# Two transformer layers on one core: woven work cut into stages by engine, and the last product's operands loaded three groups ahead

## The chip, the cores and the metric

The kernel runs on one core of one Trainium2 chip. A core has a matrix engine (PE; its weight loads are listed apart as PEld), a vector engine (DVE), a scalar engine (ACT), GpSimd (POOL) and SyncE (SP), which issues the transfers. Each engine takes its instructions strictly in the order of its own queue; semaphores tie the queues together. The metric is device time in microseconds (us): the median of several executions. One further execution was profiled, and its trace is what the prediction reads.

## The reference

The input x is one sequence of S = 2048 rows of D = 576. Two layers are applied with the same weights, each an attention and an MLP:

```
def attention(x):                      # H = 32 heads of 18
    q, k, v = split_heads(x @ wqkv)
    phi_q = concat([softmax(q @ w_phi), softmax(-(q @ w_phi))])
    phi_k = concat([softmax(k @ w_phi), softmax(-(k @ w_phi))])
    kv, z = phi_k.T @ v, sum(phi_k, rows)
    return ((phi_q @ kv) / (phi_q @ z + 1e-6)) @ wo
def mlp(x):                            # F = 4608
    return (relu(x @ w1 + b1) ** 2) @ w2 + b2
for _ in range(2):
    x = x + attention(layernorm(x))
    x = x + mlp(layernorm(x))
```

Everything is float32.

## The kernel before, in words

**Tiles.** The 2048 rows are four blocks of 512 (`TB`), a block is four tiles of 128 (`NT`). D is cut in pieces of 128 and F in 36 groups of 128 (`NF`). A float32 operand is held as a high and a low part, and a product is three matmuls: high by high, low by high, high by low. So each operand needs a "split": ACT copies the high part, and DVE or POOL subtracts it to make the low one.

**Stages.** A layer first needs the sums over all keys (`kv`), then does each block's queries, attention and MLP. In time: a barrier that finishes the keys; the MLP of one block, group by group (`g_mlp`, names `m_3` in layer 0 and `m_1` in layer 1), into which the attention of the next block and the queries and features of the third are woven (`back_first`); the MLP of the second block (`m_2` and `m_0`), into which the rest of the attention of blocks three and four is woven (`back_second`); then both MLPs of blocks three and four together (`g_pair`, names `m_p`). Their first product is made out of seven products in place of eight, which needs sums of blocks of rows: the "combined rows" t1 to t4, b11, b21 and b22, made by `g_norm_halves` and `g_norm_second` (L893 to L932 of the page). Eighteen steps of `products` do these (three PSUM banks: bx, by and bz), and the second product of one of the two blocks alongside. `seconds` then does the other block's second product: 36 groups of 15 matmuls (L1031 and L1041), whose hidden rows come back from memory (`load_high`, L1079 to L1083) and whose weights are loaded and split by `load_wide` (L996 to L1002). In layer 0 the second layer's norm, values and keys of three blocks (`back_keys`, names `n_`, `v_`, `k_`, `w_`, `kv_`) are woven into `seconds`.

**What sets the order.** `weave(main, other, rate)` writes out the order of the program: after each step of `main` it adds `rate` to an account and runs steps of `other`, each of which takes its cost from the account, while there is one unit in it. Rates and costs are constants in the code. A scheduler then keeps each engine's instructions in about the order written. A step of `other` writes out all that it needs on every engine, one after the other: a key tile's step (`g_k` with `soft_k`) writes the matmuls of the raw key, DVE's maximum and minimum (L427, L428), the subtractions (DVE L431, POOL L432), the exponential (ACT L433), the sums and reciprocal (DVE L435, L436), the scaling (POOL L443) and at once or one step later the `kv` matmuls (L471). A query tile's features are made by `g_soft` (the same to L436) and `g_phi`: products with the key sums (L589, one half on DVE and one on POOL), their reduction (L590), small rows (L591 to L594) and the scaling (L599, one half on DVE, one on POOL). The combined rows of a tile are one step: PE's transposes into a PSUM bank (L823), the sums on DVE and POOL (to L912), and five splits (ACT L922, DVE or POOL L923).

**Buffers.** While an MLP is woven, two PSUM banks (tag "w") are free for the woven work; in `seconds` three. In `seconds` the loads of group f + 2 are written behind the matmuls of group f, with two buffers each for the raw weights (`r2`), their split (`s2`) and the hidden rows' split (`hb`). In the woven MLPs, a group is the relu (ACT L731), a square and its split (ACT L732 and L733, DVE L734) between its first product (L724) and its second (L742 and L751), and the splits of its weights (ACT L709 and L710, DVE L712 and L713, POOL L714).

Of the kernel before, what the change touches and what calls it, by code (L numbers as in the profile page):

```python
# [21 lines left out]
def layers_kernel(  # L22
# [304 lines left out]
    def g_norm(x_of, dst, name, then=None):  # L327
# [15 lines left out]
        def turn(t, xn):  # L343
# [4 lines left out]
            pt = wtile(f"{name}p{t}")  # L348
            p3 = pt.rearrange("p (c n) -> p c n", n=P)
            for c in range(KC):  # L350
                nc.tensor.transpose(p3[:, c], xn[:, c * P : (c + 1) * P], ident)
# [3 lines left out]
        def turn_rest(h):  # L355

            xh = dst["h"]
            rows = slice(h * TB // 2, (h + 1) * TB // 2)
            pt = wtile(f"{name}p{NT}{h}")
            for i in range(NT // 2):  # L360
                nc.tensor.transpose(pt[:, i * P : (i + 1) * P],
                                    xd[:, h * NT // 2 + i].rearrange("p a b -> p (a b)"), ident)
            nc.scalar.activation(xh[:, KC, rows], pt[:, : TB // 2], AF.Copy)
            nc.vector.tensor_sub(xh[DT:, KC, rows], pt[DT:, : TB // 2], xh[DT:, KC, rows].bitcast(F32))

# [5 lines left out]
        yield from lagged(NT, scale, turn_all)  # L371
# [47 lines left out]
    def soft(src, name, apart=False):  # L419
# [12 lines left out]
        nc.gpsimd.tensor_sub(e4[:, 1], m[:, 1], v)  # L432
        nc.scalar.activation(e, e, AF.Exp)  # L433
        r = sb.tile([P, 2, H], F32, tag="r", name=f"{name}r", bufs=4)
        nc.vector.tensor_reduce(r, e4, op=ALU.add, axis=AX.X)  # L435
        nc.vector.reciprocal(r, r)  # L436
        return e, r

    def soft_k(src, name):
        e, r = soft(src, name)  # L440
        e3 = e.rearrange("p s (h d) -> p (s h) d", d=DH)
        r2 = r.rearrange("p s h -> p (s h)")
        nc.gpsimd.tensor_mul(e3, e3, r2.unsqueeze(2).to_broadcast([P, 2 * H, DH]))  # L443
# [137 lines left out]
    def g_phi(layer, er, ph, name, fine=False):  # L581

        zb = sums[layer]["zb"]
        for t in range(NT):
            e, r = er[t]
            u = sb.tile([P, 2, H], F32, tag="u", name=f"{name}u{t}")
            for s in range(2):
                m = sb.tile([P, D], F32, tag="qk" if fine else "x", name=f"{name}m{t}{s}", bufs=5)
                (nc.gpsimd if s else nc.vector).tensor_mul(m, e[:, s], zb[:, s])  # L589
                nc.vector.tensor_reduce(u[:, s], m.rearrange("p (h d) -> p h d", d=DH), op=ALU.add, axis=AX.X)  # L590
            nc.vector.tensor_mul(u, u, r)  # L591
            nc.vector.scalar_tensor_tensor(u[:, 0], u[:, 0], DEN_EPS, u[:, 1], op0=ALU.add, op1=ALU.add)
            nc.vector.reciprocal(u[:, 1], u[:, 0])
            nc.vector.tensor_mul(r, r, u[:, 1].unsqueeze(1).to_broadcast([P, 2, H]))  # L594
            if fine:
                yield
            for s in range(2):
                e3 = e[:, s].rearrange("p (h d) -> p h d", d=DH)
                (nc.gpsimd if s else nc.vector).tensor_mul(  # L599
                    e3, e3, r[:, s].unsqueeze(2).to_broadcast([P, H, DH]))  # L600
            ph.append(e)
            yield

# [197 lines left out]
    def g_norm_halves(x_of, name, then, main, tail, cost):  # L801
# [16 lines left out]
        for t in range(NT):  # L818
            pt = wtile(f"{name}p{t}")
            p4 = pt.rearrange("p (a c n) -> p a c n", a=2, n=P)  # L820
            for a in range(2):
                for c in range(HK):
                    nc.tensor.transpose(p4[:, a, c], xns[t][:, (a * HK + c) * P : (a * HK + c + 1) * P], ident)  # L823
            main(t, p4)
            yield cost
            if t % 2:
                pt = wtile(f"{name}p{NT}{t}")
                p3 = pt[:TP].rearrange("p (a n) -> p a n", a=2)
                for a in range(2):
                    for i in range(2):  # L830
                        nc.tensor.transpose(p3[:, a, i * P : (i + 1) * P],
                                            xd[:, t - 1 + i, a * TP : (a + 1) * TP], ident)
                tail(t // 2, p3)
                yield cost

    def g_norm_first(x_of, dst, name, then):
# [17 lines left out]
        yield from g_norm_halves(x_of, name, then, main, tail, 1.0)  # L854
# [4 lines left out]
    def g_norm_second(x_of, dst, name, then):  # L859

        ops, full = {}, []
# [53 lines left out]
        def main(t, p4):  # L915
# [4 lines left out]
            for k, src in combine((p4[:, 0], p4[:, 1]), *old):  # L920
# [4 lines left out]
        def tail(h, p3):  # L925
            cols = slice(h * TB // 2, (h + 1) * TB // 2)
            for k, src in combine((p3[:, 0], p3[:, 1]), *([f[:, cols]] for f in full)):
# [3 lines left out]
        yield from g_norm_halves(x_of, name, then, main, tail, 5.0)  # L931
        dst.update(ops)  # L932

    def g_pair(layer, blocks, x, after, name):
# [61 lines left out]
        def load_wide(f):  # L996
            r2 = sb.tile([P, D], F32, tag="r2", name=f"{name}r2_{f}")
            nc.sync.dma_start(r2, w2[(f % NF) * P : (f % NF + 1) * P])
            s2 = sb.tile([P, NC * HP], F32R, tag="s2", name=f"{name}s2_{f}")
# [77 lines left out]
        def load_high(f):  # L1077
            r = sb.tile([P, TB], F32, tag="ft", name=f"{name}g{f}", bufs=4)
            nc.sync.dma_start(r, hd[f % NF])  # L1079
            hb = sb.tile([P, 2 * D], F32R, tag="hb", name=f"{name}hc{f}")  # L1080
# [258 lines left out]
```

## Time and profile before

| what | number |
|---|---|
| median of three executions | 2571.31 us (2571.26 to 2573.71) |
| the profiled execution's own time | 2576.0 us |
| its span in the trace | 2574.2 us |
| PE busy | 2493.8 us, 97% |
| DVE, ACT, POOL busy | 64%, 51%, 38% |
| PE waits, barrier and start of the program among them | about 80 us |

The page's first part gives busy times, its second the span in 40 slices; below that, groups of instructions by line. The line numbers are those of the kernel before; the same code stands further down in the changed one (L471 is L527 there, L1041 is L1142). "Waits" are idle times of an engine put down to the instruction that released it.

### The profile page before, as it was taken

To read this page: it belongs to the slowest core of one execution; us is meant where nothing else is said; L and a number is where in the kernel's file an instruction comes from. 1 tells how busy PE (TensorE), PEld (TensorE's weight loads), DVE (VectorE), ACT (ScalarE), POOL (GpSimd) and SP (SyncE) were. 2 spreads that over 40 slices of the span, in tenths; PEclk is the share of its full clock that TensorE was granted. 3 is DMA by queue.
4 is the path that set the end of the run, shared out by engine and by line. 5 is a ranking of instruction groups with operands and counts; after the bars stand their busy time and mean duration, and the time that the engine had idled before them with its cause. 6 is when DMAs were issued, how large, how long until landed. Compare 5 with 4: busy or idle time off the path is not lost. (4 is left out here: it accounts for less than half of the span.)

```text
span 2574.2 us, 41588 instructions
## 1 busy us (share of the span) xinstructions
PE 2493.8 (97%) x15108; PEld 2185.5 (85%) x15108; DVE 1640.9 (64%) x2570; ACT 1303.3 (51%) x2293; POOL 973.6 (38%) x1101
## 2 busy tenths in 40 slices
PE   8998999999999999999899989999999999999999
PEld 8998888888887888888888988888888877888888
DVE  7778757655856655545777778475658565555444
ACT  4344545354536666654343435553455466666543
POOL 3544312312434555541334433132123345555322
PEclk9999999999999999999999999999999999999999
DMA  8103433345334433338543143233453344333265
GB/s 251 57 23 107 141 90 85 109 132 183 99 112 125 136 111 102 107 97 256 166 139 116 45 143 104 85 92 110 137 173 94 117 127 146 100 108 102 86 195 156
DMA packets 257224, 312.99 MB, mean 122 GB/s; under 512 B 29818, under 2 KB 175482, under 8 KB 254458
## 3 DMA queue, kind: packets, MB, share of 16 engines
q1 hardware_dynamic: 255760, 307.64, 39.4%
q8 instruction: 118, 1.93, 0.3%
q10 hardware_dynamic: 1258, 2.70, 0.3%
q14 instruction: 88, 0.72, 0.1%
HBM read 255.42 MB, written 54.82 MB: 121 GB/s over the span
## 5 line engine op out<-in xcount | busy, mean ns | idle before, releaser
L1002 POOL TENSOR_TENSOR m_ps<-m_pr,m_ps 128x128 fp32r<-128x128 f32 x144 | 120.0, 834 | 343.5 <-ACT m_ps L1000 289.4
L1001 DVE TENSOR_TENSOR m_ps<-m_pr,m_ps 128x448 fp32r<-128x448 f32 x144 | 97.0, 674 | 153.0 <-ACT m_ps L1000 153.0
L1041 PE MATMUL m_pacc<-m_ps,m_phb 128*128 128x448 f32 x864 | 188.5, 366 | 0.0
L1041 PEld LDWEIGHTS m_pacc<-m_ps,m_phb 128*128 128x128 f32 x864 | 162.1, 188 | 18.1
L1000 ACT ACTIVATE m_ps<-m_pr 128x576 fp32r<-128x576 f32 x144 | 97.9, 680 | 142.6 <-PE m_pacacc L1031 86.1
L1041 PE MATMUL m_pacacc<-m_ps,m_phc 128*128 128x448 f32 x648 | 147.2, 370 | 0.0
L1041 PEld LDWEIGHTS m_pacacc<-m_ps,m_phc 128*128 128x128 f32 x648 | 122.9, 190 | 10.6
L751 PE MATMUL m_2acc<-m_2s,m_2hb 128*128 128x448 f32 x432 | 100.3, 366 | 2.9 <-DVE m_2hb L734 2.9
L751 PE MATMUL m_0acc<-m_0s,m_0hb 128*128 128x448 f32 x432 | 100.1, 366 | 2.8 <-DVE m_0hb L734 2.8
L724 PE MATMUL m_0ph<-a_0nh,m_0h 128*128 128x512 f32 (+1 forms) x380 | 98.0, 385 | 4.8 <-ACT m_0hr L731 4.7
L724 PE MATMUL m_2ph<-a_2nh,m_2h 128*128 128x512 f32 (+1 forms) x380 | 98.9, 387 | 3.4 <-ACT m_2hr L731 3.3
L724 PE MATMUL m_1ph<-t1onh,m_1h 128*128 128x512 f32 (+1 forms) x380 | 99.3, 390 | 0.6 <-ACT t1onh L352 0.6
L751 PE MATMUL m_3acc<-m_3s,m_3hb 128*128 128x448 f32 x432 | 99.7, 366 | 0.0
L751 PE MATMUL m_1acc<-m_1s,m_1hb 128*128 128x448 f32 x432 | 99.4, 365 | 0.0
L724 PE MATMUL m_3ph<-t0onh,m_3h 128*128 128x512 f32 (+1 forms) x380 | 97.3, 385 | 1.4 <-DVE t0ox L681 1.4
L751 PEld LDWEIGHTS m_2acc<-m_2s,m_2hb 128*128 128x128 f32 x432 | 81.0, 188 | 14.3 <-DVE m_2hb L734 3.8
L751 PEld LDWEIGHTS m_0acc<-m_0s,m_0hb 128*128 128x128 f32 x432 | 80.9, 188 | 14.0 <-DVE m_0hb L734 3.7
L751 PEld LDWEIGHTS m_1acc<-m_1s,m_1hb 128*128 128x128 f32 x432 | 81.0, 188 | 10.4
L751 PEld LDWEIGHTS m_3acc<-m_3s,m_3hb 128*128 128x128 f32 x432 | 81.0, 188 | 10.5 <-ACT m_3hb L732 0.2
L724 PEld LDWEIGHTS m_0ph<-a_0nh,m_0h 128*128 128x128 f32 x380 | 68.0, 188 | 18.7 <-ACT m_0hr L731 6.1
L724 PEld LDWEIGHTS m_2ph<-a_2nh,m_2h 128*128 128x128 f32 x380 | 68.7, 190 | 17.3 <-ACT m_2hr L731 4.5
L724 PEld LDWEIGHTS m_1ph<-t1onh,m_1h 128*128 128x128 f32 x380 | 70.8, 195 | 14.4 <-ACT t1onh L352 0.8
(2504 smaller groups left out, 7423.8 us busy)
## 6 DMA issues: line engine op xcount, KB each, us to landing
m_pr<-in_B_w SPq DMA_DIRECT2D x144, 288.0 KB
m_pr<-in_B_w SPq DMA_DIRECT2D x72, 256.0 KB
hd<-m_pu SPq DMA_DIRECT2D x72, 256.0 KB
m_pg<-hd SPq DMA_DIRECT2D x72, 256.0 KB
m_3r<-in_B_w SPq DMA_DIRECT2D x36, 288.0 KB
m_2r<-in_B_w SPq DMA_DIRECT2D x36, 288.0 KB
m_1r<-in_B_w SPq DMA_DIRECT2D x36, 288.0 KB
m_0r<-in_B_w SPq DMA_DIRECT2D x36, 288.0 KB
```

The costliest lines, as they stand in the source:

```text
L724: nc.tensor.matmul(ph[:, cols], a, m, start=(k == 0), stop=(k == len(ops) - 1))
L751: nc.tensor.matmul(acc[t][:, :R], a[:, rows], m, start=(f == 0 and k == 0), stop=(f == NF - 1 and k == 2))
L1000: nc.scalar.activation(s2[:, :D], r2, AF.Copy)
L1001: nc.vector.tensor_sub(s2[:, D : D + R], r2[:, :R], s2[:, :R].bitcast(F32))
L1002: nc.gpsimd.tensor_sub(s2[:, D + R : 2 * D], r2[:, R:], s2[:, R:D].bitcast(F32))
L1041: nc.tensor.matmul(accs[b][t][:, :R], a[:, rows], m, start=(g == 0 and k == 0), stop=(g == NF - 1 and k == 2))
```

## The change

The arithmetic is the same but for one operation; the order of the program, the stages' costs and some buffers change.

1. A helper `pipeline(n, stages, costs)` runs item i's stage k at step i + k, the latest stage first, with a weave step between any two.
2. The features of queries (`g_features`) become five stages: start, exponential, sums and products, factors, scaling; 10.0 units a tile.
3. The combined rows become stages: transposes (0.3), sums (3.6), splits (2.4), over six items (four tiles and two pairs of tails); `g_norm_first` transposes (0.3) and splits (1.0).
4. In `products`, z is made by ACT from bx with the bias as soon as the first of two products is done, and DVE adds by to it after the second; before, ACT copied by and DVE added bx and the bias.
5. `back_keys`: norm in stages; keys as raw, start, exponential, end, an empty step, `kv`; woven at 4.0 a group, before 4.5.
6. `seconds`: the loads of group f + 3 are written ahead of the matmuls of group f. Of the groups of the last product (f from 36 on) every odd one has its raw weights in tag r1 and its split in tag h1; of its hidden rows' splits every odd one lies in two constants that are free by then (kbh, kbl).

```diff
+    def pipeline(n, stages, costs):
+        for i in range(n + len(stages) - 1):
+            for k in reversed(range(len(stages))):
+                if 0 <= i - k < n:
+                    stages[k](i - k)
+                    yield costs[k]
...
     def g_features(layer, raws, ph, name):
-        er = []
-        yield from paced(held(g_soft(raws, er, name)), 5.5)
-        yield from paced(held(g_phi(layer, er, ph, name, True)), 2.8)
+        rs, ms = {}, {}
+        def start(t):
+            ph.append(soft_parts(raws[t], f"{name}Q{t}"))
+        def add(t):
+            rs[t] = soft_sums(ph[t], f"{name}Q{t}")
+            ms[t] = phi_products(layer, ph[t], f"{name}m{t}")
+        def factors(t):
+            phi_factors(ms.pop(t), rs[t], f"{name}u{t}")
+        yield from held(pipeline(NT, (start, lambda t: soft_exp(ph[t]), add, factors, lambda t: phi_scale(ph[t], rs[t])),
+                                 (2.6, 0.4, 3.0, 2.8, 1.2)))
...
-        yield from g_norm_halves(x_of, name, then, main, tail, 1.0)
+        yield from g_norm_halves(x_of, name, then, (main,), (tail,), (0.3, 1.0))
...
-        yield from g_norm_halves(x_of, name, then, main, tail, 5.0)
+        yield from g_norm_halves(x_of, name, then, (main, split_main), (tail, split_tails), (0.3, 3.6, 2.4))
...
                 product(k, bx, "a11", "b11", True)
+                z = sb.tile([P, TB], F32, tag="hr", name=f"{name}z{f0}", bufs=2)
+                nc.scalar.activation(z, bx, AF.Identity, bias=bias(f0))
                 product(k, by, "a12", "b21", True)
-                z = sb.tile([P, TB], F32, tag="hr", name=f"{name}z{f0}", bufs=2)
-                nc.scalar.activation(z, by, AF.Copy)
-                nc.vector.scalar_tensor_tensor(z, bx, bias(f0), z, op0=ALU.add, op1=ALU.add)
+                nc.vector.tensor_add(z, by, z)
                 nc.scalar.activation(z, z, AF.Relu)
...
-            for f in range(NF, NF + 2):
+            for f in range(NF, NF + 3):
                 load_wide(f)
                 load_high(f)
             for f in range(NF, 2 * NF - 1):
+                if f + 3 < 2 * NF:
+                    load_wide(f + 3)
+                    load_high(f + 3)
                 second(f)
-                if f + 2 < 2 * NF:
-                    load_wide(f + 2)
-                    load_high(f + 2)
                 yield
...
-                    yield from paced(g_k(xk, wpair("k", f"w{m}"), es, f"k{m}",
-                                         then=lambda t: kv_tile(1, vts[t], es[t], f"kv{m}_{t}")), 3.2)
+                stages = (raw, start, lambda t: soft_exp(es[t]), end, lambda t: None)
+                if not last:
+                    stages += (lambda t: kv_tile(1, vts[t], es[t], f"kv{m}_{t}"),)
+                yield from pipeline(NT, stages, (1.0, 2.6, 0.4, 1.8, 0.1, 0.8))
...
-        weave(seconds, iter(()) if layer else back_keys(), 4.5)
+        weave(seconds, iter(()) if layer else back_keys(), 4.0)
```

Three places show what moves. The first is PE in `seconds` of layer 0, at the keys of block 3: `m_pacacc` and `m_pach` are the groups of the last product (the numbers after `m_ps` count the groups), `kv_3_2k` is the `kv` product of tile 2. Before:

```order
L471 MATMUL kv_3_2k<-k_3K2e,vs_12017 32x2x18 x32
L1041 MATMUL m_pach<-m_ps_46_12682,m_phc_12688 128x448 x3
L1041 MATMUL m_pacacc_11963<-m_ps_46_12682,m_phc_12688 128x448 x3
L1041 MATMUL m_pacacc_11964<-m_ps_46_12682,m_phc_12688 128x448 x3
L1041 MATMUL m_pacacc_11965<-m_ps_46_12682,m_phc_12688 128x448 x3
L1031 MATMUL m_pacacc_11966<-m_phc_12688,m_ps_46_12682 128x512 x3
L1041 MATMUL m_pach<-m_ps_47_12741,m_phc_12747 128x448 x3
L1041 MATMUL m_pacacc_11963<-m_ps_47_12741,m_phc_12747 128x448 x3
L1041 MATMUL m_pacacc_11964<-m_ps_47_12741,m_phc_12747 128x448 x3
L471 MATMUL kv_3_3k<-k_3K3e,vs_12018 32x2x18 x32
L1041 MATMUL m_pacacc_11965<-m_ps_47_12741,m_phc_12747 128x448 x3
```

The same place in the changed kernel, from the end of group 45, which follows the last raw key:

```order
L1132 MATMUL m_pacacc_11966<-m_phc_12504,m_ps_45_12498 128x512 x3
L527 MATMUL kv_3_0k<-k_3K0e,vs_12026 32x2x18 x32
L1142 MATMUL m_pach<-m_ps_46_12567,m_phc_12573 128x448 x3
L1142 MATMUL m_pacacc_11963<-m_ps_46_12567,m_phc_12573 128x448 x3
L1142 MATMUL m_pacacc_11964<-m_ps_46_12567,m_phc_12573 128x448 x3
L1142 MATMUL m_pacacc_11965<-m_ps_46_12567,m_phc_12573 128x448 x3
L1132 MATMUL m_pacacc_11966<-m_phc_12573,m_ps_46_12567 128x512 x3
L527 MATMUL kv_3_1k<-k_3K1e,vs_12027 32x2x18 x32
L1142 MATMUL m_pach<-m_ps_47_12600,m_phc_12606 128x448 x3
```

Group 47 follows whole, and behind it `kv_3_2k` and `kv_3_3k` one after the other. So the `kv` of tiles 0 to 2 have moved behind the last raw key by one to three groups; that of the last tile has three whole groups and three `kv` products between the raw key and itself, where it had two groups and nine matmuls of a third, and one `kv`.

The second place is ACT while the combined rows are made: `a_1n...` are splits of combined rows, `m_2...` the MLP's relu (L731), square (L732, L733) and weights (L709, L710). Before:

```order
L922 ACTIVATE a_1nt1h<-a_1nu_8318 128x2x128
L922 ACTIVATE a_1nh<-a_1nu_8318 128x2x128
L731 ACTIVATE m_2hr_8365<-m_2ph_8277,b1t 128x512
L922 ACTIVATE a_1nh<-a_1np_8313 128x2x128
L922 ACTIVATE a_1nt3h<-a_1nu_8319 128x2x128
L922 ACTIVATE a_1nt4h<-a_1nu_8319 128x2x128
L732 ACTIVATE m_2hb_8366<-m_2hr_8365 128x512
L709 ACTIVATE m_2h_27_8414<-m_2r_27_8408 128x640
```

In the changed kernel, where L1016 is the split and L812 to L814 are relu and square:

```order
L812 ACTIVATE m_2hr_8306<-m_2ph_8218,b1t 128x512
L790 ACTIVATE m_2h_26_8348<-m_2r_26_8342 128x640
L813 ACTIVATE m_2hb_8307<-m_2hr_8306 128x512
L814 ACTIVATE m_2hr_8306<-m_2hr_8306 128x512
L1016 ACTIVATE a_1nh<-a_1np_8254 128x2x128
L1016 ACTIVATE a_1nt1h<-a_1nu_8269 128x2x128
L1016 ACTIVATE a_1nh<-a_1nu_8269 128x2x128
L791 ACTIVATE m_2s_25_8285<-m_2r_25_8279 128x576
L1016 ACTIVATE a_1nt3h<-a_1nu_8270 128x2x128
L1016 ACTIVATE a_1nt4h<-a_1nu_8270 128x2x128
```

A tile's five splits and the relu have changed places: the relu stands ahead of the splits, and the split rows were summed a step earlier.

The third place is DVE while a block's features are made, with the MLP's own rows between (L712 and L713 weights, L734 the square's split). Before, at the start of tile 2's softmax:

```order
L712 TENSOR_TENSOR m_2h_12_7165<-m_2r_12_7159,m_2h_12_7165 128x640
L734 TENSOR_TENSOR m_2hb_7129<-m_2hr_7128,m_2hb_7129 128x512
L427 TENSOR_REDUCE a_1Q2m<-a_1qs_6916 128x32
L428 TENSOR_REDUCE a_1Q2m<-a_1qs_6916 128x32
L713 TENSOR_TENSOR m_2s_11_7107<-m_2r_11_7101,m_2s_11_7107 128x448
L431 TENSOR_TENSOR a_1Q2e<-a_1qs_6916,a_1Q2m 128x576
L435 TENSOR_REDUCE a_1Q2r<-a_1Q2e 128x64
```

In the changed kernel (L793, L794 and L815 are the MLP's rows, L483 the sums, L641 the product with the key sums, L470 to L474 the next tile's start, L656 the scaling):

```order
L793 TENSOR_TENSOR m_2h_14_7290<-m_2r_14_7284,m_2h_14_7290 128x640
L815 TENSOR_TENSOR m_2hb_7248<-m_2hr_7247,m_2hb_7248 128x512
L470 TENSOR_REDUCE a_1Q3m<-a_1qs_6998 128x32
L471 TENSOR_REDUCE a_1Q3m<-a_1qs_6998 128x32
L794 TENSOR_TENSOR m_2s_13_7226<-m_2r_13_7220,m_2s_13_7226 128x448
L474 TENSOR_TENSOR a_1Q3e<-a_1qs_6998,a_1Q3m 128x576
L656 TENSOR_TENSOR a_1Q0e<-a_1Q0e,a_1Q0r 128x576
L647 TENSOR_REDUCE a_1u_7277<-a_1m_7215 128x32
L647 TENSOR_REDUCE a_1u_7277<-a_1m_7216 128x32
```

The sums of a tile (L435, now L483) no longer stand right behind the subtraction that ACT's exponential waits for; other tiles' rows lie between.

More of the change, by code (lines that the diff above doesn't have):

```diff
@@ L584, in g_phi, with phi_scale @@
+    def phi_scale(e, r):
+        for s in range(2):
+            e3 = e[:, s].rearrange("p (h d) -> p h d", d=DH)
+            (nc.gpsimd if s else nc.vector).tensor_mul(
+                e3, e3, r[:, s].unsqueeze(2).to_broadcast([P, H, DH]))
+    def g_phi(layer, er, ph, name):
         for t in range(NT):
             e, r = er[t]
[L586 to L600, printed above, removed]
+            phi_factors(phi_products(layer, e, f"{name}m{t}", "x"), r, f"{name}u{t}")
@@ L798, in g_mlp, with g_norm_halves @@
             nc.sync.dma_start(out[b * TB + t * P : b * TB + (t + 1) * P] if layer else xs[b][t], x)
-    def g_norm_halves(x_of, name, then, main, tail, cost):
+    def g_norm_halves(x_of, name, then, main, tail, costs):
         xd = sb.tile([P, NT, 2 * TP], F32, tag="xd", name=f"{name}e", bufs=1)
@@ L859, in g_norm_second @@
     def g_norm_second(x_of, dst, name, then):
-        ops, full = {}, []
+        ops, full, made = {}, [], {}
         def two(t):
```

162 lines of the change are left out of this document (119 added, 43 removed).

## The prediction

> **What bounds the kernel now.** I read the page's busy times first, then PE's waits, then the stages in which they lie, then their timelines. The page says that PE is busy nearly all the time:
>
> ```profile
> span 2574.2 us, 41588 instructions
> PE 2493.8 (97%) x15108; PEld 2185.5 (85%) x15108; DVE 1640.9 (64%) x2570; ACT 1303.3 (51%) x2293; POOL 973.6 (38%) x1101
> L1041 PE MATMUL m_pacc<-m_ps,m_phb 128*128 128x448 f32 x864 | 188.5, 366 | 0.0
> ```
>
> The change takes no matmul away, so all that it can win lies in the 80.4 us in which PE is idle (2574.2 less 2493.8), and in stretches at a lower clock. PE's waits, with the total, the number and the longest:
>
> ```profile
> PE m_pach L1041 <- DVE m_ps L1001: 5.5, 2, 4.5
> PE m_0ph L724 <- ACT m_0hr L731: 4.7, 4, 2.3
> PE m_ppx L1012 <- DVE m_pz L1108: 3.8, 5, 1.4
> PE m_2ph L724 <- ACT m_2hr L731: 3.3, 2, 2.4
> PE m_ppx L1012 <- DVE m_pu L1122: 3.2, 2, 1.6
> PE kv_0k L471 <- POOL k_3K0e L443: 3.0, 1, 3.0
> PE kv_3k L471 <- POOL k_3K3e L443: 3.0, 1, 3.0
> PE kv_3k L471 <- POOL k_2K3e L443: 3.0, 1, 3.0
> PE m_2acc L751 <- DVE m_2hb L734: 2.9, 2, 1.6
> PE m_0acc L751 <- DVE m_0hb L734: 2.8, 2, 1.6
> ...
> PE m_pach L1041 <- DVE m_phc L1083: 1.2, 3, 0.4
> ...
> PE n_3p L351 <- DVE n_3n L336: 0.8, 1, 0.8
> ...
> PE n_3p L361 <- DVE n_3h L364: 0.6, 1, 0.6
> ...
> PE kv_1k L471 <- POOL k_2K1e L443: 0.2, 1, 0.2
> ```
>
> The waits at the start and in the barriers are left out here; the change doesn't reach them. The rest falls into four groups, one for each part of the change: keys beside the last product (5.5 + 3.0 + 3.0 + 3.0 + 1.2 + 0.8 + 0.6 + 0.2 = 17.3 us in 11 waits); combined rows (the relu's: 4.7 + 3.3 = 8.0 in 6); features (L734's: 2.9 + 2.8 = 5.7 in 4); products (z's: 3.8 in 5). The wait on `m_pu` stays, its code being the same.
>
> A wait costs a little more than its idle time, since the matmul behind it shows its whole length where one in a row shows a step. Nine of them in a row:
>
> ```profile
> 1238.80 2.02 PE L1041 MATMUL m_pacacc<-m_ps,m_phc 128*128 128x448 f32 x9
> 1240.66 0.86 PE L1031 MATMUL m_pacacc<-m_phc,m_ps 128*128 128x512 f32 x3
> ```
>
> One step is (1240.66 - 1238.80) / 9 = 0.207 us and one matmul's length 0.366 (the page's row), so a wait costs 0.16 us more.
>
> Some waits cost still more, for the granted clock falls behind them (the clock is the column behind POOL's). The first two rows follow a wait of `kv_0k` of 3.0 us, the third a wait of 2.4 for a relu, the fourth one of 2.3 for a relu in layer 1:
>
> ```profile
> 1228.20:1231.70 3.50, 3.50 (x74) 3.42 (x75) 1.98 (x4) 1.82 (x3) 1.55 (x2) 0.51 0.07 25
> 1231.70:1235.20 3.50, 3.50 (x26) 3.42 (x25) 2.73 (x5) 1.55 (x4) 1.49 (x2) 1.00 0.30 81
> 787.90:791.40 3.50, 3.50 (x10) 2.75 (x9) 3.04 (x8) 1.88 (x4) 0.91 (x2) 0.51 0.41 104
> 2065.40:2068.80 3.40, 3.40 (x15) 2.80 (x16) 2.56 (x6) 2.30 (x4) 0.46 (x1) 1.00 0.20 56
> ```
>
> 3.5 us at 0.51 lose 1.7 us. [...]
>
> The keys' stage has four such stretches, which its mean clock shows too (0.03 of 235 us is 7):
>
> ```profile
> 1160.00:1395.00 235.00, 217.67 (x1715) 198.13 (x1714) 163.04 (x233) 101.57 (x166) 80.27 (x80) 0.97 0.55 173
> ```
>
> So at most this can go: keys 17.3 + 11 x 0.16 + 4 x 1.7 = 25.9; combined rows 8.0 + 6 x 0.16 + one stretch, about 1.4 = 10.3; features 5.7 + 4 x 0.16 = 6.4; products 3.8 + 5 x 0.16 = 4.6. Together 47.2 us, under 2% of the run.
>
> **The change, part by part.** *Keys and the loads three deep.* The last tile of block 3 shows the chain:
>
> ```profile
> 1245.06 0.78 PE L1041 MATMUL m_pach<-m_ps,m_phc 128*128 128x448 f32 x3
> ...
> 1258.05 0.77 PE L471 MATMUL kv_3k<-k_3K3e,vs 128*32 128x36 f32 x64 [3.01 <-POOL k_3K3e L443]
> 1255.66 2.33 POOL L443 TENSOR_TENSOR k_3K3e<-k_3K3e,k_3K3r 128x1152 f32<-128x1152 f32 x1 [2.91 <-DVE k_3K3r L436]
> ```
>
> From the raw key's last matmul (1245.06) to `kv` it takes 13.0 us. By the order of the changed kernel three groups and three `kv` products lie between: 15 matmuls of 0.207 are 3.1 us, a `kv` about 0.7 (1258.05 to the next at 1258.75), so 3 x 3.1 + 3 x 0.7 = 11.4. Of the wait of 3.0 there remain 1.0 to 1.6, at this tile and its like in block 2; the waits of `kv_0k` and `kv_1k`, whose products move behind later raw keys, are gone. The 4.5 us at L1001 are a weight split that stands on DVE behind a long split of the next block's values:
>
> ```profile
> 1379.17 3.61 DVE L301 TENSOR_TENSOR w_0v0l<-w_0v0r,w_0v0h 128x1440 fp32r<-128x1440 f32 x1
> ...
> 1387.22 0.87 DVE L1001 TENSOR_TENSOR m_ps<-m_pr,m_ps 128x448 fp32r<-128x448 f32 x1
> ACT m_ps L1000 <- PE m_pacacc L1031: 20.4, 5, 7.3
> ```
>
> ACT's part of that split waits for PE to free a buffer (last row). Three deep, it is written a group (3.1 us) and more ahead, and has twice the buffers, so 4.5 becomes at most 1.4. Two tails of about 1.3 with 0.16 and a clock stretch each (2 x 3.2 = 6.4) and 0.5 elsewhere stay: 25.9 - 6.9, so **-19**. The best is -25.9. The worst is that both tail waits stay with their stretches (2 x (3.0 + 0.16 + 1.7) = 9.7), the 4.5 too (6.4), and 2 more come at `n_3n`, whose rows now stand close ahead of their transposes: -8. What is moved past: the transfers of `load_wide` and `load_high` are issued one group earlier on SP, the same number; nothing queued behind them there is waited for sooner.
>
> *Combined rows.* The relu stands on ACT behind a split whose source POOL is still summing:
>
> ```profile
> 793.04 0.74 POOL L912 TENSOR_TENSOR a_1nu<-a_1nu,a_1nb21l 128x256 f32<-128x256 f32 x1
> 793.80 0.42 ACT L922 ACTIVATE a_1nt4h<-a_1nu 128x256 fp32r<-128x256 f32 x1 [1.35 <-POOL a_1nu L912]
> 794.13 0.67 ACT L731 ACTIVATE m_2hr<-m_2ph,b1t 128x512 f32<-128x512 f32 x1
> ...
> 740.00:850.00 110.00, 106.59 (x519) 91.53 (x518) 67.71 (x118) 60.31 (x116) 51.69 (x71) 0.98 0.39 114
> ```
>
> In the changed order the relu is ahead of the splits, and those find sums written a step before. ACT's own rows don't fill the stage (60 of 110 us, last row), so what held the relu was POOL. **-9** of 10.3. If one layer's half stays, -5; beyond that see the slower rival.
>
> *Features.* Here DVE is nearly full. The window of one block's features, a wait of DVE for the exponential, three rows at the end, and a first product of the MLP from the chain of work that ended last:
>
> ```profile
> 630.00:697.00 67.00, 64.06 (x325) 55.93 (x324) 58.85 (x80) 35.21 (x57) 27.19 (x20) 1.00 0.26 77
> DVE a_1Q3r L435 <- ACT a_1Q3e L433: 2.3, 1, 2.3
> 693.16 1.69 POOL L599 TENSOR_TENSOR a_1Q3e<-a_1Q3e,a_1Q3r 128x576 f32<-128x576 f32 x1 [3.75 <-DVE a_1Q3r L594]
> 693.74 1.65 DVE L734 TENSOR_TENSOR m_2hb<-m_2hr,m_2hb 128x512 fp32r<-128x512 f32 x1
> ...
> 697.51 0.68 DVE L734 TENSOR_TENSOR m_2hb<-m_2hr,m_2hb 128x512 fp32r<-128x512 f32 x1
> ...
> 1975.52 3.26 PE m_0ph L724 x14
> ```
>
> The wait for the exponential (2.3 of DVE's 8.15 idle us, with its like at other tiles) goes, since other tiles' rows lie between subtraction and sums. But 44.4 units become 40, at 5.0 a group 8.0 groups for 8.9, with the same DVE rows of the features; the 0.9 group less holds three MLP rows a group of 0.68 (L734 alone) or more, at 0.85 about 2.3 us. So DVE has some 56.5 us to do in 8 groups. PE needs 6.4 for each: 14 matmuls of 512 columns 3.26 (last row), three more of these 0.70, and twelve of 0.207; 51.2 in all. Were it all exposed, a block would lose 5.3, 2.1 more than today's 3.2: over two layers **+5** with rounding. Against that, DVE runs into the stage ahead of PE and can fall behind by some groups' slack before PE sees it, and a row that now lies under a POOL row is stretched (1.65 against 0.68 at L734), which needn't fall on the same rows again. Best -6.4; I take **-4.4**, a left-over of 1 us a block.
>
> [...]
>
> *Products.* z's bank bx is now read by ACT behind the first product, with 14 matmuls (3 us) until PE writes it again; DVE's row, on which PE waited, reads by. That bank is needed only two products later. **-4.5** of 4.6. Worst: the five waits move to ACT's row (0 gained) and one like `m_pu`'s longest (1.6) comes on top.
>
> *New waits* I put at **+2**: the weaves end later (`back_second` 163.6 units for 158.4, at 5.0 a group 32.7 groups for 31.7, of 36), and rows that were hidden meet others.
>
> Sum: -19 - 9 - 4.5 - 4.4 + 2 = -35, so 2576.0 becomes 2541. The medians stand 4.7 below the profiled execution (2571.3), so the forecast is **2536**.
>
> **The rivals.**
> 1. *The waits move on* instead of going: features stay bound by DVE, the tails of the keys and the `n_3n` rows keep most of theirs. Keys -10, combined rows -6, products -3, features +1, others +1: -17, 2554. For it: DVE at 58.85 of 67 us and 163 of 235 in the two stages, and no work is taken from any engine.
> 2. *All of it goes*, 47: 2524. For it: ACT and POOL are at half in these stages. Against it: the 11.4 us for a chain of 13.0.
> 3. *Slower: two banks held too long.* The combined rows' transposes have two PSUM banks. Today a bank is used within one step; now it is held from the transposes over sums and splits, 6.0 units or 1.2 groups, and the transposes of item i need the bank of item i - 2. PE, in order, would stop with the MLP behind it. The price: one step's POOL work that the split must sit out is five rows (two sums, three splits by the code) of 0.74 as at L912, 3.7 us, with 0.16 and a clock stretch 5.6; four items of six, two layers: +45, and the 9 not won, against 35: +19, 2590. It decides from where the split of item i - 2 ends after PE reaches item i. Against it: PE needs 8 us for these 1.2 groups, twice the 3.7.
> 4. *Nothing comes of it*: the scheduler's order would leave the waits as they are, 2571. Against it: the order's rows did move.
>
> **How the numbers follow.** Forecast 0.60 (2536, give or take 8), rival 1 0.22, rival 2 0.06, rival 3 0.08, rival 4 0.04. The range takes the forecast, rival 1 and the upper end of the best case: 2523 to 2558; the worst ends of all four parts (-8, -5, +5, +1.6, and +2) give 2567 and are left out. About 0.2% is what a measurement of this kernel can tell from no change (5 us): faster 0.87, within it 0.04, slower 0.09.
>
> **What would show it.** In the changed profile: no wait of PE on the relu during the combined rows, none on z's row, no half clock there; at the last `kv` of blocks 3 and 2 a wait of 1 to 1.6 in place of 3.0, none at `kv_0k`; the m_pach wait below 1.5; L734 waited for at most 1 us a block. The prediction is wrong if PE waits at the combined rows' transposes, if features' waits grow, or if the barriers, which I take as unchanged, get longer, since their inputs come out of the woven stages.

## The result and the profile after

The changed kernel takes **2558.1 us** (median of four executions, 2557.6 to 2559.8) against 2571.3 before: the ratio is 0.9948, with a 95% interval of 0.9931 to 0.9965. It is faster, by 13 us; the forecast was 35 us, and the result lies just outside the range (2523 to 2558).

The page after, to be read beside the same lines of before:

```profile
span 2558.1 us, 41548 instructions
PE 2490.5 (97%) x15108; PEld 2188.9 (86%) x15108; DVE 1632.0 (64%) x2570; ACT 1306.9 (51%) x2293; POOL 967.7 (38%) x1101
```

PE's idle time is 67.6 us (2558.1 less 2490.5), where it was 80.4. The list of PE's waits shows what became of the rows that the prediction quoted. Gone are those on L734, on the relu during the combined rows, on z, and the 4.5 us on the weight split. These stand there now (waited for, total, number, longest):

```profile
PE kv_3k L527 <- POOL k_3K3e L495: 6.1, 1, 6.1
PE kv_3k L527 <- POOL k_2K3e L495: 5.0, 1, 5.0
...
PE m_1ph L805 <- ACT m_1hr L812: 2.4, 1, 2.4
PE m_3ph L805 <- ACT m_3hr L812: 2.4, 1, 2.4
PE n_3p L355 <- DVE n_3n L344: 2.4, 1, 2.4
...
PE m_ppx L1113 <- DVE m_pu L1222: 1.9, 3, 1.4
...
PE a_1qp L435 <- ACT a_1qs L453: 1.6, 1, 1.6
PE a_2qp L435 <- ACT a_2qs L453: 1.6, 1, 1.6
```

Three things stand out. The two waits for the last key tile are longer than before (6.1 and 5.0 us, where they were 3.0 each). A relu is waited for in `m_1` and `m_3`, the first woven MLPs, where the prediction named no wait. And PE waits at two raw queries (the last two rows), where it did not before.

The length of each stage is the distance between the first matmuls of its names in the two traces:

| stage | before | after | difference |
|---|---|---|---|
| all ahead of the first MLP, layer 0 | 254.6 | 256.5 | +1.9 |
| first woven MLP (m_3) | 279.5 | 282.6 | +3.1 |
| second woven MLP (m_2) | 316.3 | 308.7 | -7.6 |
| products, layer 0 | 326.4 | 323.7 | -2.7 |
| last product with the keys, layer 0 | 226.5 | 218.3 | -8.2 |
| barrier, layer 1 | 125.6 | 126.8 | +1.2 |
| first woven MLP (m_1) | 284.0 | 287.6 | +3.6 |
| second woven MLP (m_0) | 316.1 | 308.6 | -7.5 |
| products and last product, layer 1 | 445.3 | 445.3 | 0.0 |

The differences add up to the 16.1 us between the two traced executions (2574.2 and 2558.1); the medians differ by 13, for the traced execution of the kernel before was 4.7 us above its median and that of the changed kernel 1.7. The first row is taken as no effect of the change: in the 14 traces of this study that part took 253.9 to 257.2 us whatever the kernel. The combined rows and features together gave about what was forecast (15.1 for 13.4), the keys gave 8 where 19 were forecast, and the first woven MLPs, which had no term of their own in the sum, lost 6.7.

The timeline of the last key tile of block 3 shows the first miss (start, length, engine, line):

```profile
1234.26 0.77 PE L1142 MATMUL m_pach<-m_ps,m_phc 128*128 128x448 f32 x3
...
1252.37 1.19 PE L527 MATMUL kv_3k<-k_3K3e,vs 128*32 128x36 f32 x64 [6.05 <-POOL k_3K3e L495]
...
1237.59 2.64 DVE L1187 TENSOR_TENSOR m_phc<-m_pg,m_phc 128x512 fp32r<-128x512 f32 x1
1240.15 1.91 DVE L309 TENSOR_TENSOR w_2v0l<-w_2v0r,w_2v0h 128x1440 fp32r<-128x1440 f32 x1
1241.99 1.65 DVE L309 TENSOR_TENSOR w_2v1l<-w_2v1r,w_2v1h 128x1440 fp32r<-128x1440 f32 x1
1243.56 0.74 DVE L470 TENSOR_REDUCE k_3K3m<-k_3ks 128x32 f32<-128x576 f32 x1
...
1237.34 2.34 POOL L495 TENSOR_TENSOR k_3K2e<-k_3K2e,k_3K2r 128x1152 f32<-128x1152 f32 x1 [2.01 <-DVE k_3K2r L484]
...
1249.99 2.33 POOL L495 TENSOR_TENSOR k_3K3e<-k_3K3e,k_3K3r 128x1152 f32<-128x1152 f32 x1 [2.54 <-DVE k_3K3r L484]
...
1237.60 0.39 ACT L453 ACTIVATE k_3ks<-k_3kp 128x288 f32<-128x288 f32 x1
```

The raw key's last matmul ends at 1234.3 and its `kv` starts at 1252.4: 18.1 us, where before it was 13.0. PE arrives at the `kv` 12.0 us after the raw key (1246.3), where 11.4 were forecast, and waits 6.05. In those 18.1 us the tile itself is worked on for less than 10: ACT comes to its first copy only at 1237.60, DVE to its maximum at 1243.56, 9.3 us after the matmuls. Ahead of it stand tile 2's last rows, load splits of the product and two weight splits of the next block.

DVE had the same kinds of rows in that place before the change, the two weight splits among them. The first three rows are of the kernel before, the last of the changed one:

```profile
1239.19 1.35 DVE L435 TENSOR_REDUCE k_3K2r<-k_3K2e 128x64 f32<-128x1152 f32 x1 [2.26 <-ACT k_3K2e L433]
...
1245.72 1.64 DVE L301 TENSOR_TENSOR w_2v0l<-w_2v0r,w_2v0h 128x1440 fp32r<-128x1440 f32 x1
...
1248.86 0.74 DVE L427 TENSOR_REDUCE k_3K3m<-k_3ks 128x32 f32<-128x576 f32 x1
```

```profile
1234.24 1.35 DVE L483 TENSOR_REDUCE k_3K2r<-k_3K2e 128x64 f32<-128x1152 f32 x1 [1.89 <-ACT k_3K2e L479]
```

From tile 2's sums to tile 3's maximum DVE takes 9.7 us before (1239.19 to 1248.86) and 9.3 now (1234.24 to 1243.56). What moved is PE: its last raw key ended 5.9 us after those sums had started (1245.06), and now ends as they start (1234.26).

The second miss, in `m_3`:

```profile
434.26 1.44 PE L805 MATMUL m_3ph<-t0onh,m_3h 128*128 128x512 f32 x5 [2.43 <-ACT m_3hr L812]
...
432.47 1.16 ACT L479 ACTIVATE a_0Q3e<-a_0Q3e 128x1152 f32<-128x1152 f32 x1 [6.21 <-POOL a_0Q3e L475]
433.54 0.67 ACT L812 ACTIVATE m_3hr<-m_3ph,b1t 128x512 f32<-128x512 f32 x1
...
430.83 1.61 POOL L475 TENSOR_TENSOR a_0Q3e<-a_0Q3m,a_0qs 128x576 f32<-128x576 f32 x1 [0.42 <-DVE a_0Q3m L471]
```

The exponential of query tile 3, now a stage of its own, stands on ACT's queue ahead of the MLP's relu. ACT waits 6.21 us in it for POOL's subtraction, the relu behind it starts at 433.54, though its product had ended at 428.7, and PE stands still. It is the very pattern that the change took away at the combined rows, with another instruction in front.

Windows of the clock (the column behind POOL's) and of DVE in the changed kernel:

```profile
434.30:437.60 3.30, 3.30 (x14) 2.71 (x15) 2.37 (x4) 2.27 (x4) 0.87 (x1) 1.00 0.17 49
1699.10:1702.50 3.40, 3.40 (x9) 2.67 (x8) 3.04 (x6) 1.09 (x2) 0.90 (x1) 0.50 0.43 110
1252.40:1255.30 2.90, 2.90 (x69) 2.65 (x70) 2.60 (x5) 0.00 (x0) 1.58 (x2) 0.50 0.36 108
1328.30:1333.90 5.60, 5.60 (x76) 5.06 (x77) 2.58 (x5) 0.00 (x0) 1.56 (x2) 0.50 0.61 198
424.00:431.00 7.00, 7.00 (x34) 6.04 (x33) 7.00 (x14) 1.60 (x3) 2.52 (x3) 1.00 0.31 89
```

Behind both `kv_3k` waits the clock is at half (2.9 and 5.6 us, 4.3 lost). In the last row DVE is busy 7.0 of 7.0 us ahead of the wait in `m_3`.

### The profile page after: what moved, and what is told of

The parts are those of the page before. It is cut to its first block, busy times and chain, and to the rows that moved or that the text cites. A ratio compares the mean times of both kernels' runs of the same rounds, so it can differ in the third digit from the quotient of the medians.

```text
span 2558.1 us, 41548 instructions
## 1 busy us (share of the span) xinstructions
PE 2490.5 (97%) x15108; PEld 2188.9 (86%) x15108; DVE 1632.0 (64%) x2570; ACT 1306.9 (51%) x2293; POOL 967.7 (38%) x1101
## 5 line engine op out<-in xcount | busy, mean ns | idle before, releaser
L1142 PEld LDWEIGHTS m_pacc<-m_ps,m_phb 128*128 128x128 f32 x864 | 162.1, 188 | 18.1
L1123 DVE TENSOR_TENSOR m_phb<-m_pz,m_phb 128x512 fp32r<-128x512 f32 x72 | 56.5, 785 | 115.8 <-ACT m_pz L1122 114.3
L832 PEld LDWEIGHTS m_1acc<-m_1s,m_1hb 128*128 128x128 f32 x432 | 81.0, 188 | 10.3
L805 PEld LDWEIGHTS m_3ph<-t0onh,m_3h 128*128 128x128 f32 x380 | 69.5, 192 | 17.6 <-ACT m_3hr L812 3.3
```

Of the source, the lines that this page charges most:

```text
L805: nc.tensor.matmul(ph[:, cols], a, m, start=(k == 0), stop=(k == len(ops) - 1))
L832: nc.tensor.matmul(acc[t][:, :R], a[:, rows], m, start=(f == 0 and k == 0), stop=(f == NF - 1 and k == 2))
L1123: nc.vector.tensor_sub(hl, r, hh.bitcast(F32))
L1142: nc.tensor.matmul(accs[b][t][:, :R], a[:, rows], m, start=(g == 0 and k == 0), stop=(g == NF - 1 and k == 2))
```

## The experiments

Each kernel is the changed one with the edit shown, unless another is named; times are medians, ratios those to the kernel before (2572 to 2573 us in these groups), with a 95% interval.

**The last `kv` later (`kv_late`).** The last tile's `kv` product is kept back and written behind the next block's norm.

```diff
+            late = []
...
+                while late:
+                    kv_tile(*late.pop())
...
-                    stages += (lambda t: kv_tile(1, vts[t], es[t], f"kv{m}_{t}"),)
+                    def put(t):
+                        args = (1, vts[t], es[t], f"kv{m}_{t}")
+                        late.append(args) if t == NT - 1 else kv_tile(*args)
+                    stages += (put,)
```

> The changed kernel, but the kv product of a block's last tile is written behind the next block's norm, four groups later. Theory: the two waits of PE at kv_3k (6.05 and 5.04 us) are the last tile's own chain (18.1 us from the raw key's last matmul to its kv, where three groups and three kv products give 11.4), so PE finds the keys ready and both waits go, with the half clock that begins around them: 11.1 + 2 x 0.16 + 4.5 = 15.9 us less, 2542. Rival: the chain is limited by DVE and POOL work that PE must wait for in any case, so the wait comes back at the next norm's transposes or at a weight split: under 5 us less, 2553 to 2558.

Measured 2546.0 us, ratio 0.9899 (0.9884 to 0.9914): 12 below the changed kernel. The stage takes 206.5 us for 218.3. Neither `kv_3k` wait is left; what came in their place is small:

```profile
PE n_2p L369 <- DVE n_2h L377: 1.2, 1, 1.2
...
PE n_2p L355 <- DVE kv L535: 0.8, 1, 0.8
...
PE n_0p L355 <- DVE n_0l L364: 0.5, 1, 0.5
```

So the waits go as the theory has it: PE has other work, and what DVE and POOL still do for the last tile costs little once nobody asks for it at once. The size was put too high, 12 us for 15.9: the three new waits are 2.5 of the difference.

**Old features in the first MLP alone (`first_old`).** `g_features_old` has the code of the kernel before.

```diff
-            mid = (g_queries(layer, order[2], None, later, m), g_features(layer, later, early, m))
+            mid = (g_queries(layer, order[2], None, later, m), g_features_old(layer, later, early, m))
```

> The changed kernel with the old features (softmax in one step, denominators in two) in the first woven MLP of each layer only. Theory: the exponential as a stage of its own stands on ACT ahead of the MLP's relu and waits 6.2 us for POOL's subtraction; without it the two relu waits of 2.43 us and the half clock behind one of them go, 2 x 2.6 + 1.7 = 6.9 us less, 2551. Rival: these waits come from another order of the weave as a whole (rate 3.7), and the old features put a wait elsewhere in the same stage: same as the changed kernel, 2558, within 2.

Measured 2549.3 us, 0.9911 (0.9896 to 0.9926), 9 below the changed kernel. The waits on the relu are gone, and the first MLPs take 277.9 and 283.1 us for 282.6 and 287.6: 9.2 together, more than the two waits and the half clock behind one of them (6.9). In the runs `late_old` and `best` below, with the same old features there, these MLPs take 279.4 to 279.5 and 283.5 to 283.6, so some 2 us of the 9.2 vary from trace to trace. The theory holds.

**Loads two deep (`two_deep`).** The loads as before the change, all else changed.

> The changed kernel with loads of the last product two groups deep, as before the change. Theory: the last tile's chain is long because ACT and DVE hold other tiles' rows ahead of it, of which a group's load splits are only a part; the waits at kv_3k shrink by the 1.2 to 2.4 us of load splits on ACT, to 4 or 5 us each, and part of the 4.5 us at the weight split comes back: 2554 to 2562. Rival: the third group's load splits are what lengthened the chain by 5 us, then the kv_3k waits fall back to 3.0 or below and the stage gets 6 us shorter, 2552, if the 4.5 us do not come back.

Measured 2562.1 us, 0.9955 (0.9939 to 0.9972), and both theories missed how: the waits at `kv_3k` are not smaller, they are gone, and others stand in their place.

```profile
PE m_pach L1139 <- DVE m_ps L1099: 10.0, 6, 4.5
```

```profile
1247.71 1.60 PE L1139 MATMUL m_pach<-m_ps,m_phc 128*128 128x448 f32 x2 [2.28 <-DVE m_ps L1099]
...
1246.08 1.58 DVE L1099 TENSOR_TENSOR m_ps<-m_pr,m_ps 128x448 fp32r<-128x448 f32 x1
```

The same DVE row stands at the same place of the queue, behind the last tile's start; with a group less in hand PE needs its result a group earlier and stops there, 7 us ahead of the `kv`, then runs slowly: the nine matmuls from 1249.11 on take 3.56 us, where the nine from 1241.65 on took 1.99. Meanwhile the tile gets done: its chain is 18.7 us, as long as with three groups. So with the staged keys the depth of the loads doesn't lengthen the chain; it decides at which of DVE's rows PE stops. Against two groups the changed kernel wins 6 us in this stage (224.3 to 218.3).

**Old key steps (`keys_old`).** The norm and the keys as before at 4.5 a group, the loads three deep.

> The changed kernel with the old norm and the old key steps at 4.5 a group in the last product, and the loads three deep. Theory: the waits of the kernel before return at kv_0k and kv_3k (3.0 each, three of them, half a clock behind each), without the 4.5 us at the weight split: the stage takes 226.6 - 6.4 = 220 us where it takes 218.3 with the staged keys, 2560. Rival: three-deep loads lengthen any key's chain, then the kv waits are 5 us or more here too, 2566.

Measured 2561.0 us, 0.9956 (0.9941 to 0.9971), the theory's time within 1, which is partly luck, since the stage takes 223.9 us for the 220 expected. The waits:

```profile
PE kv_3k L527 <- POOL k_2K3e L495: 6.3, 1, 6.3
...
PE kv_3k L527 <- POOL k_3K3e L495: 3.6, 1, 3.6
...
PE kv_0k L527 <- POOL k_3K0e L495: 3.0, 1, 3.0
```

The wait of the load splits, gone with three groups, has in part gone into `kv_3k`: 6.3 in block 2 for 3.0. So with the old keys and three groups the chain of block 2 is longer, 15.5 us for 14.0, and that of block 3 is not; why was not followed up. Together with the two runs above: each part alone (staging the keys with two groups, three groups with the old keys) shortens the stage by 2.2 to 2.6 us, both together by 8.2, and with the last `kv` moved by 20.

**Weight splits held back (`hold_w`).** The next block's weight splits may be issued only behind the last tile's raw copies (ACT) and reciprocal (DVE).

```diff
+                    with ExitStack() as behind:
+                        if b != order[0]:
+                            for key in ("copy", "sums"):
+                                behind.enter_context(tc.issue_after(dense[key].ins))
+                        vpiece = wpair("v", f"w{m}")
...
```

The weights of the last block's keys are held back in the same way.

> The changed kernel, but the next block's weight splits (ACT 1.40 each, DVE 1.91 and 1.65) may be issued only behind the last key tile's raw copies on ACT and its reciprocal on DVE. Theory: these splits, which the scheduler puts ahead of the last tile's maximum, make 3.4 of the 5 us by which the tile's chain grew; the waits at kv_3k become 2.6 and 1.6 us, about 7 us of idle time and 2 us of half clock less: 2549, from 2547 to 2552. Rival: DVE's sum of work up to that place is what counts, and the same splits are then waited for elsewhere in the stage: above 2554.

Measured 2554.5 us, 0.9933 (0.9921 to 0.9945): at the rival's edge. The chain became 16.8 and 16.2 us for 18.1 and 17.1, not 14.7. Rows of its timeline tell why:

```profile
1249.46 0.88 PE L527 MATMUL kv_3k<-k_3K3e,vs 128*32 128x36 f32 x64 [4.69 <-POOL k_3K3e L495]
...
1242.95 1.35 DVE L483 TENSOR_REDUCE k_3K3r<-k_3K3e 128x64 f32<-128x1152 f32 x1 [2.26 <-ACT k_3K3e L479]
...
1246.04 3.37 POOL L495 TENSOR_TENSOR k_3K3e<-k_3K3e,k_3K3r 128x1152 f32<-128x1152 f32 x1 [2.02 <-DVE k_3K3r L484]
```

DVE came to the tile 3.4 us earlier, as expected, but then stood idle 2.26 for the exponential, which other rows had filled; and the scaling on POOL, now beside the weight split on DVE, took 3.37 us for 2.33. The share of 3.4 in 5 us that the theory gave to the splits was wrong: holding them back shortens the chain by 1.3, and they stood ahead of the tile's maximum in the kernel before too.

**Both corrections (`late_old`)**, the last `kv` later and old features in the first MLPs.

> Both corrections of the changed kernel together: a block's last kv product behind the next block's norm, and the old features in the first woven MLP of each layer. Theory: the two lie in different stages and add up: 2546 less the 8.8 us that the old features won (2558.1 to 2549.3), 2537. Rival: one of them only moved PE's waiting to a resource that the other needs too, and the sum is less than 4 us better than the better one, above 2542.

Measured 2537.8 us, 0.9867 (0.9853 to 0.9880). They add up.

**One part alone.** `a_only` and `b_only` are the kernel before with the staged features, or the staged combined rows, and nothing else of the change.

> The kernel before with the staged features alone. Theory: in the second woven MLPs the waits on L734 go (3.2 us a layer) and a wait at the queries of 1.8 comes, 1.4 us less a layer; in the first woven MLPs the exponential ahead of the relu costs what the changed kernel shows, 3.1 and 3.6 us more: 4 us above the kernel before. Rival: the stages of the features pay in both MLPs by themselves, and the losses come from other parts of the change: 2 to 6 us below.

Measured 2577.4 us, 1.0018 (1.0009 to 1.0027): the staged features alone make the kernel slower, by the 4 us of the theory.

```profile
PE m_2ph L805 <- ACT m_2hr L812: 3.2, 2, 2.3
PE m_0ph L805 <- ACT m_0hr L812: 3.1, 2, 2.3
...
PE m_3ph L805 <- ACT m_3hr L812: 2.4, 1, 2.4
PE m_1ph L805 <- ACT m_1hr L812: 2.4, 1, 2.4
```

The relu's waits of the combined rows stay, as they must, and the two new ones come; the second woven MLPs win 1.6 and 1.5 us.

> The kernel before with the staged combined rows alone. Theory: the relu's waits go (8.0 us in 6, with 0.16 each and one stretch of half clock), 10 to 12 us below the kernel before. Rival: the gain in the second woven MLPs came from the features; then no more than 5 us below.

Measured 2555.7 us, 0.9928 (0.9911 to 0.9945), more than expected: 9.5 and 9.4 us in the two second MLPs, for the waits on L734 are gone as well, with the old features in place. This one part is at least as fast as the whole change (2558.1). That the waits on L734 went asked for the next run.

**One constant (`phase`)**, the kernel before with

```diff
-        yield from g_norm_halves(x_of, name, then, main, tail, 1.0)
+        yield from g_norm_halves(x_of, name, then, main, tail, 1.3)
```

> The kernel before with one number changed: the first combined rows cost 1.3 a step and not 1.0, 1.8 units more in all, as the staged version does, so that the features behind them start a third of a group later. Theory: the four waits on L734 hang on where in a group the features fall, not on how they are written: they go, 5.7 + 0.6 us, 2566 to 2567. Rival: they stay, and it was the staging of the combined rows that took them away: 2571 to 2574.

Measured 2567.0 us, 0.9976 (0.9967 to 0.9986). None of the four waits on L734 is left; those on the relu stay, two for each layer:

```profile
PE m_0ph L724 <- ACT m_0hr L731: 3.3, 2, 2.3
PE m_2ph L724 <- ACT m_2hr L731: 3.2, 2, 2.3
```

So these four waits were a matter of where in a group the features fell. The stages were not needed for them.

**Exponential behind the square (`exp_hold`).**

```diff
-                                 (2.6, 0.4, 3.0, 2.8, 1.2)))
+                                 (2.6, 0.4, 3.0, 2.8, 1.2)), ("last", "squared"))
```

> The changed kernel, but the stages of the features may be issued only behind the MLP's square on ACT of the group before them, so that the exponential stands behind relu and squares. Theory: the cost of the staged features in the first woven MLPs is the exponential ahead of the relu: the waits of 2.43 go with their half clock, 2 x 2.6 + 1.7 = 6.9 us less, and perhaps the two of 1.6 at the queries: 2548 to 2552. Rival: DVE is what runs late there (7.0 of 7.0 us busy ahead of the first wait), and PE then waits for the square's split in place of the relu: 2555 or more.

Measured 2548.0 us, 0.9902 (0.9888 to 0.9917), 10 below the changed kernel. The exponential now stands behind relu and squares, no relu is waited for, and the first MLPs take 277.7 and 282.6 us. DVE has the same rows to do, some of them in another order, and is just as full there: 7.00 of 7.00 us from 417 to 424 and 6.90 of 7.00 from 424 to 431, with no wait of PE. So it was the place on ACT's queue, not DVE's load, that cost these 10 us. Two rows of ACT show the new order, the square's last row and behind it an exponential that waits for nothing:

```profile
419.75 0.64 ACT L814 ACTIVATE m_3hr<-m_3hr 128x512 f32<-128x512 f32 x1
420.29 1.15 ACT L479 ACTIVATE a_0Q2e<-a_0Q2e 128x1152 f32<-128x1152 f32 x1
```

The two waits at the queries stay (1.6 each): there the exponential stands ahead of a raw query's copy and not of a relu.

**The best version (`best`)**: the changed kernel with the last `kv` later and the old features everywhere.

> The changed kernel with the last kv product behind the next norm, and with the old features everywhere, the second woven MLPs too. Theory: staged features cost there too, for the combined rows alone leave a second woven MLP of 306.8 us where the changed kernel takes 308.6: 1.9 us a layer less than with the old features in the first MLPs only (2537.8), 2534. Rival: the staged features win back what the old ones lose on L734 in this weave, 2537 to 2541.

Measured **2534.8 us**, 0.9849 (0.9835 to 0.9864), the fastest version together with the next one, 38 us below the kernel before in its group. Of the change it keeps the staged combined rows, the staged keys, the loads three deep and z's edit. PE is busy 98%, with 50.3 us of idle time:

```profile
span 2532.2 us, 41547 instructions
...
PE 2481.9 (98%) x15108; PEld 2182.9 (86%) x15108; DVE 1647.8 (65%) x2570; ACT 1306.4 (52%) x2293; POOL 984.8 (39%) x1101
```

**The same without z's edit (`best_z`).**

> As the run before it in this group, but with z as before the change (ACT copies by, DVE adds bx and the bias). Theory: z's edit is worth its five waits, 3.8 + 5 x 0.16 = 4.6 us: 2538.5. Rival: with the combined rows staged, z's waits are nearly gone without it (one of 0.38 us in the run with the combined rows alone), and the edit is worth under 1.5 us: 2534 to 2535.5.

Measured 2534.8 us, 0.9850 (0.9835 to 0.9865): no difference. With the edit PE waits in this place for DVE's row on u, without it for the one on z. The first row is of `best`, the second of `best_z`:

```profile
PE m_ppx L1120 <- DVE m_pu L1229: 1.8, 2, 1.3
```

```profile
PE m_ppx L1120 <- DVE m_pz L1219: 1.0, 3, 0.4
```

The five waits on z of before (3.8 us) are down to 1.0 without the edit. Why the staged combined rows do that to the products, which follow them, was not tried and stays open.

## Why the prediction was wrong, point by point

**Keys, -19 forecast, -8.2 measured: the step that failed.** The prediction took the 13.0 us from the raw key to its `kv` out of the old order and set it against 11.4 us of PE's work in the new one, so that of the wait of 3.0 there would remain 1.0 to 1.6. The 11.4 was nearly right: PE waited 6.05 of the 18.1 us and had covered the other 12.0. The 13.0 was not a length of the chain that carries over. It held how far DVE was behind PE at that moment. From the tile's maximum to its `kv` it took 9.2 us before and 8.8 now; the growth lies ahead of the maximum, which comes 9.3 us after the raw key's last matmul for 3.8 before in block 3, and 8.3 for 4.8 in block 2.

The rows show why. In the new order a block's raw keys stand closer together on PE, since the `kv` products have moved behind them: from the first raw key to the last it takes 23.6 us for 30.1 in block 3, and 20.5 for 25.7 in block 2. DVE has the same rows to do for them and falls behind. In block 3 the old wait of 3.0 at `kv_0k` belonged to this: across it DVE's delay behind the raw key fell from 4.9 us at tile 1 to 0.65 at tile 2 (from the raw key's last matmul to the maximum), and with the wait gone it grows from tile to tile: 1.6, 3.1, 5.2, 9.3. Idle time on PE in block 3's keys was 6.4 us before (3.0, 0.4, 3.0) and is 6.05 now. No run held the raw keys apart on PE, so this account rests on the rows of two traces. `two_deep` shows that the staged chain takes 18.7 us with two groups too, `hold_w` that holding back the weight splits takes 1.3 off it, and `kv_late` that it needn't be short, only not asked for: 206.5 us for the stage, 20 below before.

The wait on the weight split went as forecast (4.5 to none), and the one at `n_3n` came as its worst case had it (2.4 for 2).

**New waits, +2 forecast, +6.7 in the first woven MLPs alone.** This is the second step that failed. The prediction looked at the features only in the second MLPs, where they had waits, and never asked what a stage of its own does to the exponential in the first ones. `first_old` and `exp_hold` show the cause: the exponential ahead of the relu on ACT's queue, 9 and 10 us by these runs. The order of the changed kernel, which the prediction had, holds these rows.

**Features, -4.4 forecast: the waits went, but not by the stages.** `phase` takes the waits on L734 away with one constant and `b_only` without staged features; alone (`a_only`) the staged features make the kernel 4 us slower. The prediction argued from DVE's load, 58.85 of 67 us (its worst end there, 2 x 2.1, makes 4.2 and not 5). Beside the staged combined rows the staged features cost 1.8 us in each second MLP (308.6 us for the 306.8 of `b_only`), with a wait of 1.6 at the queries. So it was luck that the combined rows and features together came near their forecast: the first alone win 18.9 us, and the second take 3.8 of it away. In the changed trace a DVE row is long beside POOL: L1187 takes 2.64 us where it lies beside POOL's L495, and ends at 1240.23, 0.55 behind it; the median of its 34 rows from 1160 to 1395 is 0.69. Whether this is why the staged features win nothing was not tried.

**Combined rows, -9 forecast: right.** The relu's waits went, and with them the half clock behind one of them (0.51 from 787.9 to 791.4 before; 1.00 over 740 to 850 in the changed kernel). PE's waits at the combined rows' transposes are the same as before (1.0 at `a_0np` and `a_3np`, 0.3 at `a_0np` and `a_2np`), which settles the slower rival. `phase`, which lost the waits on L734 alone, takes 312.6 us in each second MLP and `b_only` 306.8: 11.6 us for the two, where 10.3 was the most that was forecast.

**Products, -4.5 forecast, -2.7 in layer 0 and none in layer 1.** The waits on z went and some came on u (1.9 us). `best` and `best_z` show that the edit is worth nothing by then.

**What was taken as unchanged** moved by 3 us: the start by +1.9, within the spread of 14 traces, and the barrier by +1.2, where the 14 traces lie between 125.5 and 127.5.

## What to carry to other kernels

A measured wait is not a property of the instruction that is waited for. It also depends on how far the engine that waits has run ahead of the slower queue. Take an earlier wait away, or work that stood between, and the next place where the slower queue is asked shows it: here the 3.0 us at `kv_0k` went, and the wait at the same block's `kv_3k` grew from 3.0 to 6.05. So for a chain beside other work, count the rows that stand ahead of it in the new order on each engine, and do not carry its length over from the old trace. The last item of a pipeline had no successor to hide behind here; moving what consumes it into the next phase won 12 us. And where a long instruction gets a stage of its own on an in-order engine, look at what stands behind it in that queue (here a relu, behind an exponential that waited 6.21 us) before looking at the engine's load.

## What was not expected of the hardware

The clock behind a wait could not be told from that wait's length here. The same wait for a relu in `m_3` was 2.43 us in the changed kernel (up to 434.3) and 2.39 in `hold_w` (up to 430.1). In the changed kernel full clock followed (1.00 in the first row of the windows above), in `hold_w` half:

```profile
430.90:434.20 3.30, 3.30 (x9) 2.60 (x8) 2.94 (x5) 1.47 (x3) 0.90 (x1) 0.50 0.32 91
```

In `m_1` the same wait of 2.43 was followed by 0.50 in the changed kernel too (second row of the windows above):

```profile
1697.86 1.48 PE L805 MATMUL m_1ph<-t1onh,m_1h 128*128 128x512 f32 x5 [2.43 <-ACT m_1hr L812]
```

The 14 matmuls behind that wait took 4.91 us in `m_1` (1697.86 to 1702.77) and 3.37 in `m_3` (434.26 to 437.63), with the same shapes: 1.5 us between two waits of one length. So a gap of 2.4 us could not be priced from its length alone in these traces. What else decides it was not shown.
